# Spectral filter beside a gated MLP: who copies the first transposes, where the next statistics stand, and how wide the first pass is

## Chip, cores, metric

The kernel runs on one core of a Trainium2 chip. The metric is the device time of one execution in microseconds (us). The core has five engines that run their own instruction queues in order and wait for each other through semaphores: TensorE (PE, matrix products, with PEld for its weight loads), VectorE (DVE), ScalarE (ACT), GpSimd (POOL) and SyncE (SP, which here only issues DMA transfers). PE writes to PSUM, a memory of eight banks; a bank must have been read out before PE may write to it again.

## What is computed

The rows of `A_x` (2048 rows of 512) are normalized. The result goes through two branches that are added to `A_x`: a two-dimensional FFT multiplied by a filter and transformed back, and a gated MLP with a tanh GELU.

```python
def _A_ref(x, w_r, w_i):
    B, S, D = x.shape
    X = jnp.fft.rfft2(x.astype(jnp.float32), axes=(-2, -1))
    X = X * (w_r + 1j * w_i)
    return jnp.fft.irfft2(X, s=(S, D), axes=(-2, -1)).astype(jnp.bfloat16)

def _B_ref(x, w_gate, w_up, w_down):
    g = jnp.einsum("bsd,df->bsf", x, w_gate)
    u = jnp.einsum("bsd,df->bsf", x, w_up)
    h = _gelu(g) * u
    return jnp.einsum("bsf,fd->bsd", h, w_down)

x = A_x
xn = _layernorm(x, axis=-1)
return x + _A_ref(xn, A_w_r, A_w_i) + _B_ref(xn, B_w_gate, B_w_up, B_w_down)
```

Here S = 2048, D = 512, and the MLP's inner width is 1792. All data is bfloat16, sums are float32.

## The kernel before

**Tiles.** The 2048 rows are 16 tiles of 128 rows; four tiles make a block of 512. The inner width is 14 slices (`fc`) of 128. A tile is loaded (`load_x`, `load_xc`), its mean and variance are taken on DVE (`ln_stats`, L421 and L422; the second tile in two halves, L428 and L430), the reciprocal root of the variance is formed (tiles 0 and 1: square root on ACT, L433, and reciprocal on DVE, L437; later tiles: POOL, `ln_rstd`, L442 and L443), and the tile is normalized on DVE (`ln_apply`, L450). PE then transposes it in 128 x 128 squares, and the transposed rows are copied from PSUM to `xnT`: tiles 0 and 1 one at a time (`transpose_first`, L465, with the copies at L471 on DVE or L473 on ACT), tiles 2 and 3 together and tiles 4 to 7 together (`transposes`, L490, with one copy on DVE, L497, and one on ACT, L499), later tiles by DMA.

**Units.** A `geglu_unit(b, fc, a, w)` makes `w` columns of slice `fc` of block `b`: four matmuls with the gate weights into one PSUM bank and four with the up weights into the next (both at L561), GELU on ACT from the first bank into a buffer `gg` (L573, three buffers in turn), and the product of that with the second bank on DVE into `hT` (L581). The banks come from a ring: `ring_first` has the six banks 0, 1, 2, 7, 5, 6 in this order, `ring_gu` the three banks 0, 1, 2 from its own start. A unit takes the next two banks of its ring, and waits until what was in them has been read.

**Block 0.** Its rows are not all there at the beginning, so it is done in narrower passes: slices 0 to 2 (`NQUARTER` = 3) on tile 0 alone and then on tile 1 alone, 128 columns each; slices 3 to 6 (up to `NHALF` = 7) on both, 256 columns; then slices 0 to 6 on tiles 2 and 3, 256 columns. The transposes of tiles 2 and 3 come in between, after the unit with `fc == NHALF - 2`. From slice 7 on the units are 512 wide and come from a list (`fillers`), one for each call of `filler()`. After the first of these the four tiles 4 to 7 are normalized, two more follow, and then come the transposes of tiles 4 to 7.

**Weights.** Gate and up weights come in six pieces of columns, `WPIECES` = (0, 128), (128, 384), (384, 640), (640, 896), (896, 1280), (1280, 1792), so slices 7 to 9 lie in piece 4. All loads are issued in a fixed order at the start, most by SP: tiles 0 and 1, gate pieces 0 to 2, and so on down to piece 4 after the four tiles of block 1 (`load_xc(1)`); the first two up pieces are issued by ACT.

**The order of work** is that of the calls at the end of the kernel: each call appends its instructions to the queues of the engines, and each queue is kept in order. ACT's queue at the start: square root for tile 0, square root for tile 1, then a GELU on a single column (L826) whose only purpose is to load the GELU table early, and then the first units' GELUs. PE fills its time before the first tile with 39 matmuls on zeros (`warm_up`, L541).

After block 0's beginning the same list of units is spread between the spectral branch's steps (`unit_A` L634, `unit_d` L660, `unit_B`, `unit_c`, `unit_e`, `unit_fin`), the folds on POOL (`half_fold`, L521) and DVE (`mirror_fold`, L526), and the down projections (L607).

Of the kernel before, what the change touches and what calls it, by code (L numbers as in the profile page):

```python
# [8 lines left out]
ALU = mybir.AluOpType  # L9
# [8 lines left out]
P = 128  # L18
# [209 lines left out]
def bass_parallel_sum__spectral_gfnet__glu_gated_geglu__prompt_kernel(  # L228
# [19 lines left out]
    sch = _Sched()  # L248

    with ExitStack() as es:  # L250

        def sb(name, shape, dt=BF16):
            return es.enter_context(nc.sbuf_tensor(name, shape, dt))
# [6 lines left out]
        hT = [sb("hT%d" % i, [P, NFC, 512]) for i in range(2)]  # L260
# [54 lines left out]
        gu_bank = sp_bank = bank_of  # L315
# [4 lines left out]
        def sp_bank_bf(slot):  # L320
            return ps_bf[:, slot * 1024:(slot + 1) * 1024]
# [6 lines left out]
        ring_first = _Ring((0, 1, 2, 7, 5, 6), bank_readers)  # L328
# [91 lines left out]
        def ln_stats(j):  # L420
            ev = sch.op("dve", lambda e: e.bn_stats(st[:, j, :], x_sb[:, j, :]), deps=[ev_x[j]])  # L421
            ev_ag[j] = sch.op("dve", lambda e: e.bn_aggr(ag[:, j, :], st[:, j, :]), deps=[ev])  # L422
# [3 lines left out]
        def ln_stats_half(h):  # L426

            ev = sch.op("dve", lambda e: e.bn_stats(st1[:, h, :], x_sb[:, 1, h * HD:(h + 1) * HD]), deps=[ev_x[1]])  # L428
            if h == 1:
                ev_ag[1] = sch.op("dve", lambda e: e.bn_aggr(ag[:, 1, :], st1[:]), deps=[ev])  # L430

        def ln_sqrt(a, b):
            return sch.op("act", lambda e: e.activation(rstd[:, a:b], ag[:, a:b, 1], ACT.Sqrt, bias=eps_t[:], scale=1.0),  # L433
                          deps=[ev_ag[b - 1], ev_eps])

        def ln_recip(a, b, ev):
            ev = sch.op("dve", lambda e: e.reciprocal(rstd[:, a:b], rstd[:, a:b]), deps=[ev])  # L437
            for j in range(a, b):
                ev_rstd[j] = ev

        def ln_rstd(a, b):
            ev = sch.op("pool", lambda e: e.tensor_scalar(rstd[:, a:b], ag[:, a:b, 1], LN_EPS, None, ALU.add), deps=[ev_ag[b - 1]])  # L442
            ev = sch.op("pool", lambda e: e.tensor_tensor(rstd[:, a:b], rstd[:, a:b], half_t[:, 0:b - a], ALU.pow), deps=[ev, ev_half])  # L443
            for j in range(a, b):
                ev_rstd[j] = ev
# [3 lines left out]
        def ln_apply(j):  # L449
            ev_xn[j] = sch.op("dve", lambda e: e.tensor_scalar(xn[:, j, :], x_sb[:, j, :], ag[:, j, 0:1], rstd[:, j:j + 1],  # L450
                                                             ALU.subtract, ALU.mult), deps=[ev_rstd[j], ev_ag[j]])

        ev_xnT = {}

        def transpose_first(j, eng):

            evs = []
            for h in range(2):
                slot, bdeps = ring_tr.alloc(1)
                bank = sp_bank_bf(slot)[:, 0:HD].rearrange("p (r s) -> p r s", r=2)  # L460

                def f_tr(e, h=h, bank=bank):
                    ins = None
                    for r in range(2):
                        ins = e.transpose(bank[:, r, :], xn[:, j, (2 * h + r) * P:(2 * h + r + 1) * P], ident)  # L465
                    return ins

                ev_t = sch.op("pe", f_tr, deps=[ev_id, ev_xn[j]] + bdeps)
                dst, src = xnT[:, 2 * h:2 * h + 2, j * P:(j + 1) * P], bank
                if eng == "dve":  # L470
                    ev = sch.op("dve", lambda e, dst=dst, src=src: e.tensor_copy(dst, src), deps=[ev_t])  # L471
                else:
                    ev = sch.op("act", lambda e, dst=dst, src=src: e.activation(dst, src, ACT.Copy), deps=[ev_t])  # L473
                ring_tr.add_reader(slot, ev)
                evs += [ev, ev]
            ev_xnT[j] = evs
# [55 lines left out]
        gg_readers = [[] for _ in range(NGG)]  # L532
        hT_readers = [[], []]
        ev_h_block = {}
# [8 lines left out]

            hT_readers[1].append(sch.op("pe", f, deps=[ev_zero, ev]))

        def geglu_unit(b, fc, a=0, w=512, ring=None):

            k = geg["k"]
            geg["k"] = k + 1
            s2 = k % NGG  # L550
            hb = b % 2
            ring = ring or ring_gu
            pieces = [i for i, (lo, hi) in enumerate(WPIECES) if lo < (fc + 1) * P and fc * P < hi]
            evw, evw_up = ([ev_w[i, q] for i in pieces] for q in range(2))
            evx = [ev_xnT[4 * b + i] for i in range(a // P, (a + w) // P)]
            gslot, gdeps = ring.alloc(1)

            def mm(e, wsb, slot, dcs=range(NDC)):
                ins = None
                for dc in dcs:  # L560
                    ins = e.matmul(gu_bank(slot)[:, 0:w], wsb[:, dc, fc * P:(fc + 1) * P], xnT[:, dc, b * 512 + a:b * 512 + a + w],  # L561
                                   start=(dc == 0), stop=(dc == NDC - 1))
                return ins

            if b == 0 and fc == 0 and a == 0:
                for dc in range(NDC):
                    ev_gm = sch.op("pe", lambda e, dc=dc: mm(e, wg_sb, gslot, (dc,)), deps=evw + [x[dc] for x in evx] + gdeps)
            else:
                ev_gm = sch.op("pe", lambda e: mm(e, wg_sb, gslot), deps=evw + evx + gdeps)
            uslot, udeps = ring.alloc(1)  # L570
            ev_um = sch.op("pe", lambda e: mm(e, wu_sb, uslot), deps=evw_up + udeps)
            gg = gg_sb[s2][:, 0:w]
            ev_gg = sch.op("act", lambda e: e.activation(gg, gu_bank(gslot)[:, 0:w], ACT.Gelu_apprx_tanh),  # L573
                           deps=[ev_gm] + gg_readers[s2])
            gg_readers[s2] = []
            ring.add_reader(gslot, ev_gg)
            hdeps = []
            if fc == 0 and a == 0:
                hdeps = list(hT_readers[hb])
                hT_readers[hb] = []  # L580
            ev_h = sch.op("dve", lambda e: e.tensor_tensor(hT[hb][:, fc, a:a + w], gu_bank(uslot)[:, 0:w], gg, ALU.mult),  # L581
                          deps=[ev_um, ev_gg] + hdeps)
            ring.add_reader(uslot, ev_h)
            gg_readers[s2].append(ev_h)
            ev_h_block.setdefault(b, []).append(ev_h)

        ev_acc = {}

# [224 lines left out]
            finished(j, ev_o)  # L813


        NQUARTER, NHALF = 3, 7
        ln_stats(0)
        ev_sq = ln_sqrt(0, 1)
        ln_stats_half(0)
# [2 lines left out]
            warm_up(n, ev)  # L822
        ln_apply(0)
        ln_stats_half(1)
        ev_sq = ln_sqrt(1, 2)
        sch.op("act", lambda e: e.activation(warm[:], eps_t[:], ACT.Gelu_apprx_tanh), deps=[ev_eps])  # L826
        transpose_first(0, "dve")
        ln_recip(1, 2, ev_sq)
        ln_apply(1)
        for fc in range(NQUARTER):  # L830
            geglu_unit(0, fc, 0, P, ring_first)
            if fc == 0:
                transpose_first(1, "act")
                ln_stats(2)
        ln_stats(3)
        for fc in range(NQUARTER):
            geglu_unit(0, fc, P, P, ring_first)
        ln_rstd(2, 4)
        for fc in range(NQUARTER, NHALF):
            geglu_unit(0, fc, 0, 256, ring_first)  # L840
            if fc == NQUARTER:
                ln_apply(2)
                ln_apply(3)
                half_fold(0)
            if fc == NHALF - 2:
                transposes(2, 4, ring_tr)
# [18 lines left out]
        def filler(n=1):  # L865
            for _ in range(n):
                u = next(fill, None)
                if u is None:
                    return
                todo["left"] -= 1  # L870
                if u[0] == "g":
                    geglu_unit(u[1], u[2])
                else:
                    down_unit(u[1], u[2])

        filler()
        for j in range(4, 8):
            ln_apply(j)
        filler(2)
        transposes(4, 8, ring_tr)  # L880
        half_fold(1)
        filter_i = load_filter("wi", wi_sb, A_w_i)
# [104 lines left out]
```

## Time and profile before

| | us |
|---|---|
| median of 3 runs | 180.57 (180.46 to 180.92) |
| the profiled execution, its time | 179.84 |
| its span, first to last instruction | 178.1 |

| engine | busy us | share of the span |
|---|---|---|
| PE | 174.0 | 98% |
| PEld | 98.6 | 55% |
| DVE | 116.6 | 65% |
| ACT | 87.1 | 49% |
| POOL | 55.1 | 31% |

The 16 DMA engines are busy nine tenths or more of the time in the slices from the second to the tenth (4.45 us a slice), and their rate there is 308 to 379 GB/s for the second to the sixth. A timeline line reads: start, duration, engine, line, operation, output and inputs, shapes, count, and in brackets how long the engine sat idle before it and what ended that. Starts are counted from the span's start. Lines with a `q` behind the engine's name are issues of DMA transfers. Matmul durations overlap; the distance of their starts tells what one costs.

### The profile page before, as it was taken

The page shows a single profiled execution, that of the slowest core. Times are in us where ns is not written, and L with a number is a line of the kernel's source. Part 1 is how long each engine was busy: PE and PEld are TensorE (multiplying, and loading weights), DVE is VectorE, ACT ScalarE, POOL GpSimd, SP SyncE. Part 2 cuts the span into 40 slices and gives each one's busy share as a digit, 9 for nine tenths or more (in the row PEclk, how much of TensorE's full clock was granted, in tenths as well). Part 3 has the DMA queues.
Part 4 walks back from the last instruction along what each step waited for, and adds up shares of the span by engine and source line. Part 5 has one row for each costly group of instructions (what it writes and reads, how often), then busy time and mean ns, then how long its engine had stood idle before and what let it go on. Part 6 is the DMA issues. An engine that isn't in the chain of part 4 may idle for free.

```text
span 178.1 us, 3198 instructions
## 1 busy us (share of the span) xinstructions
PE 174.0 (98%) x1157; PEld 98.6 (55%) x1157; DVE 116.6 (65%) x256; ACT 87.1 (49%) x164; POOL 55.1 (31%) x54
## 2 busy tenths in 40 slices
PE   7899999999999999999999999999999999999995
PEld 7788755555555554444554555554455555555543
DVE  2787986878767636545586886872338868885731
ACT  3635337777463634156374765723166546662100
POOL 0047253326390000000000000000008969997760
PEclk9999999999999999999999999999999999999999
DMA  5999999999997793913344494965500111111101
GB/s 150 308 338 379 372 371 171 199 169 218 231 174 192 143 296 103 305 64 88 94 105 120 91 241 75 243 139 117 118 4 29 59 59 33 60 67 47 39 29 59
DMA packets 38576, 27.15 MB, mean 152 GB/s; under 512 B 7712, under 2 KB 37792, under 8 KB 38432
## 3 DMA queue, kind: packets, MB, share of 16 engines
q1 hardware_dynamic: 34192, 24.95, 56.1%
q10 hardware_dynamic: 4368, 2.00, 5.6%
q8 instruction: 9, 0.15, 0.4%
q14 instruction: 7, 0.06, 0.2%
HBM read 17.48 MB, written 6.30 MB: 134 GB/s over the span
## 4 chain that ended last, share of the span: by engine, by line
PE 94%; ACT 2%; DVE 1%; DMA 1%; issue 0%
PE ps L561 54%; PE ps L607 27%; PE ps L740 2%; PE ps L660 2%; PE ps L634 2%; PE ps L792 2%; PE ps L771 2%; PE ps L709 2%; DMA x_sb<-in_A_x_dram 1%; PE ps L490 1%; ACT L826 1%; DVE st L421 0%; ACT rstd L433 0%; ACT xnT L473 0%; DVE bufA L450 0%
## 5 line engine op out<-in xcount | busy, mean ns | idle before, releaser
L561 PE MATMUL ps<-xnT,wg_sb 128*128 128x512 bf16 (+2 forms) x264 | 59.2, 347 | 0.7 <-DVE xnT L471 0.4
L561 PE MATMUL ps<-xnT,wu_sb 128*128 128x512 bf16 (+2 forms) x264 | 59.2, 347 | 0.2
L581 DVE TENSOR_TENSOR hT<-ps,gg 128x512 bf16<-128x512 f32 (+2 forms) x66 | 39.5, 605 | 23.9 <-PE ps L561 23.0
L607 PE MATMUL ps<-wd_sb,hT 128*128 128x512 bf16 (+2 forms) x238 | 50.7, 366 | 0.0
L573 ACT ACTIVATE gg<-ps 128x512 bf16<-128x512 f32 (+2 forms) x66 | 35.0, 532 | 24.8 <-PE ps L561 21.5
L806 POOL TENSOR_TENSOR bufC<-bufC 128x256 bf16<-128x256 f32 x16 | 14.7, 916 | 84.2 <-DVE bufC L803 84.2
L561 PEld LDWEIGHTS ps<-xnT,wu_sb 128*128 128x128 bf16 x264 | 25.0, 98 | 24.2 <-issue 0.3
L607 PEld LDWEIGHTS ps<-wd_sb,hT 128*128 128x128 bf16 x238 | 22.5, 98 | 23.4
L561 PEld LDWEIGHTS ps<-xnT,wg_sb 128*128 128x128 bf16 x264 | 23.7, 98 | 15.2 <-DMA wg_sb<-in_B_w_gate_dram 0.5
L618 DVE TENSOR_TENSOR x_sb<-ps,x_sb 128x512 bf16<-128x512 f32 (+2 forms) x17 | 11.2, 660 | 24.2 <-PE ps L607 24.2
L521 POOL TENSOR_TENSOR bufC<-bufA 128x1024 bf16<-128x1024 bf16 x8 | 16.8, 2124 | 8.6 <-DVE bufA L450 8.6
L810 POOL TENSOR_TENSOR x_sb<-x_sb,bufC 128x512 bf16<-128x512 bf16 x16 | 18.7, 1169 | 2.3
L745 ACT ACTIVATE Vp<-ps 128x514 bf16<-128x514 f32 x16 | 9.5, 599 | 15.3 <-PE ps L740 15.3
L776 ACT ACTIVATE bufA<-ps 128x512 bf16<-128x512 f32 x16 | 9.4, 597 | 14.6 <-PE ps L771 14.6
L668 ACT ACTIVATE bufB<-ps 128x512 bf16<-128x512 f32 x16 | 11.9, 744 | 9.5 <-PE ps L660 9.5
L421 DVE BATCH_NORM_STATS2 st<-x_sb 128x6 f32<-128x512 bf16 x15 | 10.2, 683 | 2.3 <-DMA x_sb<-in_A_x_dram 2.3
L802 DVE TENSOR_TENSOR bufC<-bufC,ps 128x256 f32<-128x256 f32 x16 | 6.7, 421 | 5.3 <-ACT bufC L799 5.3
L641 ACT ACTIVATE tmp<-ps 128x512 bf16<-128x512 f32 x9 | 5.4, 597 | 6.1 <-PE ps L634 6.1
L442 POOL TENSOR_SCALAR rstd<-ag 128x4 f32<-128x4 f32 (+1 forms) x4 | 1.3, 316 | 21.3 <-DVE ag L422 21.3
L714 ACT ACTIVATE Xc<-ps 128x514 bf16<-128x514 f32 x12 | 7.0, 595 | 1.0 <-PE ps L709 1.0
L799 ACT ACTIVATE bufC<-ps 128x256 f32<-128x256 f32 x16 | 6.0, 378 | 2.6 <-PE ps L792 2.6
L806 DVE TENSOR_TENSOR bufC<-bufC 128x256 bf16<-128x256 f32 x16 | 6.8, 424 | 0.5
(52 smaller groups left out, 137.5 us busy)
## 6 DMA issues: line engine op xcount, KB each, us to landing
stage_g<-Vp SPq DMA_DIRECT2D x16, 128.5 KB, 3.3
bufC<-stage_p SPq DMA_DIRECT2D x4, 512.0 KB, 5.2
out_dram<-x_sb SPq DMA_DIRECT2D x15, 128.0 KB, 1.7
wd_sb<-in_B_w_down_dram SPq DMA_DIRECT2D x1, 1792.0 KB, 15.3
stage_p<-bufB SPq DMA_DIRECT2D x7, 256.0 KB, 5.7
wr_sb<-in_A_w_r_dram SPq DMA_DIRECT2D x6, 257.0 KB, 10.7
wi_sb<-in_A_w_i_dram SPq DMA_DIRECT2D x6, 257.0 KB, 10.2
JX<-Xc SPq DMA_DIRECT2D x24, 64.2 KB, 2.6
```

The source lines that it names most:

```text
L421: ev = sch.op("dve", lambda e: e.bn_stats(st[:, j, :], x_sb[:, j, :]), deps=[ev_x[j]])
L521: ev_hf[m] = [sch.op("pool", lambda e, t=t, op=op: e.tensor_tensor(half[:, m, t, :, :], rows[:, 0, :, :], rows[:, 1, :, :], op), deps=deps ...
L561: ins = e.matmul(gu_bank(slot)[:, 0:w], wsb[:, dc, fc * P:(fc + 1) * P], xnT[:, dc, b * 512 + a:b * 512 + a + w], start=(dc == 0), stop=(d ...
L573: ev_gg = sch.op("act", lambda e: e.activation(gg, gu_bank(gslot)[:, 0:w], ACT.Gelu_apprx_tanh), deps=[ev_gm] + gg_readers[s2])
L581: ev_h = sch.op("dve", lambda e: e.tensor_tensor(hT[hb][:, fc, a:a + w], gu_bank(uslot)[:, 0:w], gg, ALU.mult), deps=[ev_um, ev_gg] + hdeps)
L607: ins = e.matmul(bank(slot)[:, 0:w], hT[hb][:, fc, jj * P:(jj + 1) * P], wd_sb[:, fc, cs], start=(fc == 0), stop=(fc == NFC - 1))
L618: ev_a = sch.op("dve", lambda e, slot=slot, cs=cs, w=w: e.tensor_tensor(x_sb[:, j, cs], bank(slot)[:, 0:w], x_sb[:, j, cs], ALU.add), deps ...
L668: ev_T[j] = sch.op("act", lambda e: e.activation(dst, src, ACT.Copy), deps=[ev_p])
L745: ev_v = sch.op("act", lambda e: e.activation(Vp[sv][:], sp_pair(slot), ACT.Copy), deps=[ev_p] + Vp_readers[sv])
L776: ev_ZT[j] = sch.op("act", lambda e: e.activation(ZT[:, :, j, :], src, ACT.Copy), deps=[ev_p] + [ev_xnT[i][0] for i in (11, 15)])
L806: y = [sch.op(("dve", "pool")[h], lambda e, h=h, op=op: e.tensor_tensor(rS[s2][:, h * HD:(h + 1) * HD], yeS[s2][:, 0, :], yeS[s2][:, 1, :] ...
L810: ev_o = sch.op("pool", lambda e: e.tensor_tensor(x_sb[:, j, :], x_sb[:, j, :], rS[s2], ALU.add), deps=[a, b, ev_xn[j]] + ev_acc.get(j, []))
```

## The change

Four edits in block 0 (line numbers of the functions behind it shift by 2 to 7).

- `transpose_first` takes one engine for each of a tile's two copies. Tile 0's are now copied by ACT and DVE (before: both by DVE), tile 1's by DVE both (before: both by ACT). Tile 0's call moves ahead of the second tile's square root in the order of calls.
- `geglu_unit` can hand its product back instead of appending it (`late=True`). The first unit's product is appended after tile 1's copies, so that DVE has the copies first.
- The statistics of tiles 2 and 3 move on DVE's queue: from behind the first and the third product to behind the fourth and the sixth.
- `NHALF` is 8 instead of 7: slice 7 of block 0 is done in two units of 256 columns in the passes instead of one of 512. The transposes of tiles 2 and 3 stand one unit later with it. One unit fewer is left in the list, and `filler(2)` ahead of the transposes of tiles 4 to 7 becomes `filler()`.

```diff
-        def transpose_first(j, eng):
+        def transpose_first(j, engs):
 
             evs = []
-            for h in range(2):
+            for h, eng in enumerate(engs):
...
-        def geglu_unit(b, fc, a=0, w=512, ring=None):
+        def geglu_unit(b, fc, a=0, w=512, ring=None, late=False):
...
-            hdeps = []
-            if fc == 0 and a == 0:
-                hdeps = list(hT_readers[hb])
-                hT_readers[hb] = []
-            ev_h = sch.op("dve", lambda e: e.tensor_tensor(hT[hb][:, fc, a:a + w], gu_bank(uslot)[:, 0:w], gg, ALU.mult),
-                          deps=[ev_um, ev_gg] + hdeps)
-            ring.add_reader(uslot, ev_h)
-            gg_readers[s2].append(ev_h)
-            ev_h_block.setdefault(b, []).append(ev_h)
+
+            def product_h():
+                hdeps = []
+                if fc == 0 and a == 0:
+                    hdeps = list(hT_readers[hb])
+                    hT_readers[hb] = []
+                ev_h = sch.op("dve", lambda e: e.tensor_tensor(hT[hb][:, fc, a:a + w], gu_bank(uslot)[:, 0:w], gg, ALU.mult),
+                              deps=[ev_um, ev_gg] + hdeps)
+                ring.add_reader(uslot, ev_h)
+                gg_readers[s2].append(ev_h)
+                ev_h_block.setdefault(b, []).append(ev_h)
+
+            if late:
+                return product_h
+            product_h()
...
-        NQUARTER, NHALF = 3, 7
+        NQUARTER, NHALF = 3, 8
...
         ln_stats_half(1)
+        transpose_first(0, ("act", "dve"))
         ev_sq = ln_sqrt(1, 2)
         sch.op("act", lambda e: e.activation(warm[:], eps_t[:], ACT.Gelu_apprx_tanh), deps=[ev_eps])
-        transpose_first(0, "dve")
         ln_recip(1, 2, ev_sq)
         ln_apply(1)
-        for fc in range(NQUARTER):
+        product_h = geglu_unit(0, 0, 0, P, ring_first, late=True)
+        transpose_first(1, ("dve", "dve"))
+        product_h()
+        for fc in range(1, NQUARTER):
             geglu_unit(0, fc, 0, P, ring_first)
-            if fc == 0:
-                transpose_first(1, "act")
-                ln_stats(2)
-        ln_stats(3)
         for fc in range(NQUARTER):
             geglu_unit(0, fc, P, P, ring_first)
+            if fc in (0, 2):
+                ln_stats(2 + fc // 2)
         ln_rstd(2, 4)
...
         filler()
         for j in range(4, 8):
             ln_apply(j)
-        filler(2)
+        filler()
         transposes(4, 8, ring_tr)
```

## Prediction

> **What bounds the kernel now.** I read the page first (busy shares, chain), then the windows, then the chain and the timeline of the first 30 us, where every edit lies.
>
> ```profile
> span 178.1 us, 3198 instructions
> PE 94%; ACT 2%; DVE 1%; DMA 1%; issue 0%
> ```
>
> ```profile
> 14.00:22.00 8.00, 8.00 (x68) 6.32 (x66) 7.01 (x18) 3.54 (x9) 3.81 (x4) 1.00 1.06 377
> ...
> 27.00:175.00 148.00, 148.00 (x912) 78.09 (x911) 96.20 (x200) 74.85 (x136) 45.58 (x41) 1.00 0.56 124
> ```
>
> In the windows the first number after the length is PE's busy time: from 14 us on PE is busy 8.00 of 8.00 and 148.00 of 148.00 us. So whatever PE's queue gains or loses in the first 27 us reaches the end nearly whole, and all that counts is when PE issues. The chain of waits from 5 to 30 us shows where PE does stand still:
>
> ```profile
> 5.99 1.28 ACT L826
> ...
> 7.65 0.56 ACT xnT L473 x2
> 8.21 0.05 issue
> 8.26 0.64 PE ps L561 x8
> 8.89 0.27 DVE hT L581
> 9.16 0.05 issue
> 9.21 1.28 PE ps L561 x16
> 10.49 0.07 issue
> 10.56 2.34 PE ps L561 x20
> ```
>
> Comparing PE's starts with its pitch (0.056 us for a 128-column matmul, 0.109 for 256, from back-to-back starts) gives stalls of 0.53 (before 6.02, for the first tile's copies), 0.21 (before 6.68, second tile's normalization), 0.45 (before 8.26: ACT copies the second tile, behind the table load), 0.27 (9.21: a product freeing its PSUM bank), 0.23 (10.56: the same, the product queued behind statistics) and 0.07 (14.13).
>
> **The change, part by part.** Times are those of the profiled execution.
>
> *First tile, one copy each.* The first pair of transposes releases its copy at 5.56. Now that copy is DVE's, over at 5.87, the second one at 6.07. On ACT such a copy takes 0.38 (L473), so it ends about 5.95, DVE's about 6.03. The first product starts 0 to 0.08 later than at 6.02: no gain. The copy now sits ahead of the second square root on ACT: back-to-back copies start 0.26 apart, so the root moves from 5.68 to 5.84, and the reciprocal, the second normalization and its transposes by 0.16; the table load and first GELU move by the same 0.16.
>
> *Second tile on DVE, before the first product.* Transposes at 6.84, DVE copies (0.29, pitch 0.21) end at about 7.7, while PE works on units 1 and 2 until 7.97 (3 units of 8 x 0.056). The 0.45 wait is gone: the second quarter starts at 7.97 instead of 8.26. With the statistics behind the fourth and sixth products, the 0.27 and 0.23 waits go as well: the sixth unit ends at 9.31, where now unit four of the wide kind starts at 9.89. A gain of 0.58 so far, and 0.81 after the 10.56 wait is gone.
>
> *Statistics later.* The third tile's now begin after the fourth product, about 9.0, the fourth's after the sixth, about 10.2 to 11.1 (0.69 + 0.18 each); POOL's rstd (1.04 from 10.32 to 11.36 now) ends about 12.2, the two normalizations (0.72) at 13.0. The transposes moved one unit later in the loop (`NHALF - 2` is now 6) would be reached by PE at 12.81, so they wait 0.26, to 13.07, and end at 13.51.
>
> *Eight units in the first pass: the weight piece.* Next on PE is unit fc=7 on tiles 0 and 1, formerly first touched at 20.24. It lies in weight piece 4 (columns 896 to 1280), whose DMAs are issued and land thus (issue times from the timeline, last column of the DMA view is us to landing):
>
> ```profile
> 7.26 0.43 SPq L341 DMA_DIRECT2D wg_sb<-in_B_w_gate_dram  x1
> 7.74 0.70 SPq L341 DMA_DIRECT2D wu_sb<-in_B_w_up_dram  x1
> ```
>
> ```profile
> wg_sb<-in_B_w_gate_dram SPq DMA_DIRECT2D x1, 384.0 KB, 6.3
> wu_sb<-in_B_w_up_dram SPq DMA_DIRECT2D x1, 384.0 KB, 7.0
> ```
>
> Gate weights land at 13.6, up weights at 14.75. Nothing that the change touches is ahead of them in SP's or ACT's queue, so they land then again. PE would want the up weights at 14.08: it waits to about 14.80, the up product takes 4 x 0.109, and the second pass starts at 15.24. Before it started at 14.13 with half a unit (0.87) less done: 15.24 - 0.87 - 14.13 = +0.24 us late. The whole gain of the opening (0.81, less 0.26) is swallowed, and any slip there below 0.67 would be too.
>
> The rate behind it: in the window 2.20 to 14.75 the DMA engines moved 323 GB/s at a busy share above 1. The Trainium skill ("Perfetto Trace Analysis", Roofline) puts one core's ceiling at about 435 GB/s; by that the same bytes would be there at about 11.5 and the wait would not exist (an estimate from that page). The trace's landing decides against it.
>
> *Eight units: PSUM bank.* The second pass is 8 units of 0.87: 15.24 + 6.98 = 22.22, against 21.97 before for the same work (fc 0 to 7 whole; the eighth as two halves costs 1.75 instead of 1.73). The next unit, fc=8, takes ring banks 0 and 1 from the start of `ring_gu`. `ring_first` has six banks in turn, two a unit: before, 17 units left banks 0 and 1 to the last but one; now the 19th unit, just finished, has them. So fc=8 waits for that unit's GELU. In the profile
>
> ```profile
> 14.13 0.60 PE L561 MATMUL ps<-xnT,wg_sb 128*128 128x256 bf16 x4
> ...
> 14.77 0.38 ACT L573 ACTIVATE gg<-ps 128x256 bf16<-128x256 f32 x1 [0.50 <-PE ps L561]
> ```
>
> a unit's GELU ends 1.02 after its gate starts; with 0.05 to PE that is 1.07, the unit is 0.87: +0.20. fc=8 starts at 22.42, 0.45 late.
>
> *`filler(2)` becomes `filler()`: normalizations 4 to 7.* They stand in DVE's queue behind the product of the unit before. Then PE had two 512-wide units until the transposes, now one:
>
> ```profile
> 20.24 1.03 PE L561 MATMUL ps<-xnT,wg_sb 128*128 128x512 bf16 x4
> ...
> 22.17 0.69 DVE L581 TENSOR_TENSOR hT<-ps,gg 128x512 bf16<-128x512 f32 x1
> ...
> 22.78 1.37 DVE L450 TENSOR_SCALAR bufA<-x_sb,ag,rstd 128x512 bf16<-128x512 bf16 x4
> ...
> 25.42 1.06 PE L490 MATMUL ps<-small,bufA 128*128 128x128 bf16 x16
> ```
>
> A wide unit's product starts 1.93 after the unit (20.24 to 22.17), the last normalization ends 1.98 after that, 0.05 to PE: 3.96. Two wide units take 3.45 (21.97 to 25.42). Now the transposes come just two units after fc=8 starts: they are reached at 25.87 and ready at 22.42 + 3.96 = 26.38: a wait of +0.51, where before there was a cover of 20.24 + 3.96 = 24.20 against 25.42, 1.2 us. DVE's queue bears this: the two mirror folds ahead (1.29) end by 24.2, before the product at 24.35. POOL's rstd for these tiles (1.04) ends about 22.5, in time.
>
> **Sum:** +0.24 (weights) + 0.20 (bank) + 0.51 (normalizations) = +0.95, with nothing after it to take it back. Profiled execution: span 178.1 + 0.95 = 179.05; its time 179.84 + 0.95 = 180.8. The median shown is 180.57, 0.73 above the profiled one, so 181.5. The bounds of the unknown: the landing can shift (at 14.0 or earlier, limited by tile 2 and 3's copies at 14.5, the first term becomes -0.50; 0.5 later, +0.74); the last two terms stand on durations of the same instructions and I give them 0.1 each.
>
> **Rivals.** This kernel's measurement tells about 0.3% (0.54 us) from no change.
>
> 1. *The up weights come in time* (by 14.0). Place: the tenth unit; it decides from 14.75 - 14.0 = 0.7 us earlier landing. Then the second pass starts at 14.5: -0.50 + 0.20 + 0.51 = +0.2, 180.8: not slower by what can be told. For it: unprofiled executions need not have this landing. Against: 323 GB/s at full DMA share, and no transfer ahead was removed. 0.16.
> 2. *The transposes don't wait*, because DVE gets to the normalizations half a microsecond sooner: +0.45, 181.0. For it: nothing but that product and folds overlap by 0.1 each. Against: DVE takes its queue in order, the product waits for PE. 0.06.
> 3. *The opening's gain reaches the end*: the 0.81 saved up to 10.56 stays on PE's queue, and neither later wait shows because the landing is early and DVE keeps its old cover: 179.8. It needs piece 4 by 13.5, and the fence above shows that cover taken away. 0.04.
> 4. *PE's clock falls in the new stalls.* The profile grants full clock in all 40 slices; the warm-up matmuls from 0.97 to about 5.0 run at 0.107 pitch, half speed, so one more such stretch costs 2 us: 183.5. Against: the 0.53 stall before 6.02 is followed by 0.056 pitch at once, and the new ones are 0.7 and 0.5. 0.03. The Trainium skill ("TensorE: Matmul & The Clock Gate", Part 1) puts the drop behind an idle window of about 3.4 us, but also reports micro-idles between groups as a second cause; by the first rule there is none here, by the second the rival's 2 us.
>
> **How the numbers follow.** The forecast has 0.71 and is 181.5, its own spread 181.1 to 182.0. The range reaches to rival 1's 180.8 and upward to 182.1 for a landing 0.5 later. Slower: the forecast, rival 4 and a little of rival 2, 0.76; same: the rest of rivals 1 and 2, 0.19; faster: rival 3 and the lower edge of 1, 0.05.
>
> **What would show it.** Right: the second quarter at about 8.0 with no ACT copy before it; PE idle before the up matmuls of the tenth unit, released by the up weights near 14.8; a gap of 0.2 before the first 512-wide unit, released by ACT's GELU; a gap of 0.5 before the 16 transposes, released by DVE L450, near 26.4. From there every PE start about 0.95 later than before. Wrong: piece 4 landed before 14.1, or the transposes follow the matmuls without a gap.

## The result, and the profile after

The changed kernel takes 181.65 us (median of 6 runs, 181.52 to 182.02), the kernel before 180.78 beside it (6 runs, 180.46 to 181.0): a ratio of 1.0052, 95% interval 1.0038 to 1.0066. The forecast was 181.5. Here and below the ratio is not the quotient of the two medians; it differs from it by up to 0.0013. Ratios leave out two executions in a slow state, one of e2 (184.27) and one of e8 (183.58).

The profiled execution of the changed kernel took 181.52, its span is 179.7. That of the kernel before, 179.84, lies below all six of its runs (180.46 to 181.0); the 1.6 us between the two spans is therefore not the effect. This matters below.

The page's head after, then the waits of PE from 12 to 30 us (who waited for what: us in total, times, longest):

```profile
span 179.7 us, 3217 instructions
...
PE 89%; SPq 4%; DMA 4%; DVE 1%; issue 0%
```

```profile
PE ps L561 <- DMA wu_sb<-in_B_w_up_dram: 0.5, 1, 0.5
PE ps L490 <- DVE bufA L450: 0.3, 1, 0.3
PE ps L561 <- DMA wg_sb<-in_B_w_gate_dram: 0.3, 1, 0.3
```

The chain that ended last now has 4% of issues on SP's queue and 4% of a weight load in it, which it had not before. The chain of waits from 5 to 30 us shows where:

```profile
8.34 0.04 issue
8.38 7.05 DMA wu_sb<-in_B_w_up_dram
15.43 0.04 issue
15.48 7.60 PE ps L561 x68
23.07 0.04 issue
23.11 1.92 PE ps L561 x8
25.03 0.02 issue
25.05 0.69 DVE hT L583
25.74 0.82 DVE bufA L450 x3
26.57 0.06 issue
26.62 0.42 DVE bufA L450
27.04 0.05 issue
27.09 1.07 PE ps L490 x16
```

Read from the top: the up weights of piece 4, issued at 8.38, land at 15.43; PE goes on at 15.48. Then 68 matmuls without a stop, a break until 23.11, one 512-wide unit, and the chain leaves PE: the unit's product on DVE, the normalizations behind it, and only then the transposes. PE's timeline at these three places:

```profile
14.39 0.61 PE L561 MATMUL ps<-xnT,wg_sb 128*128 128x256 bf16 x4 [0.35 <-DMA wg_sb<-in_B_w_gate_dram]
...
15.48 0.61 PE L561 MATMUL ps<-xnT,wu_sb 128*128 128x256 bf16 x4 [0.48 <-DMA wu_sb<-in_B_w_up_dram]
15.92 0.60 PE L561 MATMUL ps<-xnT,wg_sb 128*128 128x256 bf16 x4
...
22.47 0.60 PE L561 MATMUL ps<-xnT,wu_sb 128*128 128x256 bf16 x4
...
23.11 1.04 PE L561 MATMUL ps<-xnT,wg_sb 128*128 128x512 bf16 x4
...
25.71 1.03 PE L561 MATMUL ps<-xnT,wu_sb 128*128 128x512 bf16 x4
...
27.09 1.07 PE L490 MATMUL ps<-small,bufA 128*128 128x128 bf16 x16 [0.35 <-DVE bufA L450]
```

The brackets count from a matmul's modelled end; from the starts the stalls are longer. The last unit's up matmuls start at 22.47 and need 4 x 0.109: 22.91, and the next start is 23.11, so 0.20. The up matmuls at 25.71 need 4 x 0.216: 26.57, next start 27.09, so 0.51 (with unrounded starts). The tenth unit waits twice for weights of piece 4: its gate matmuls, reached at 13.87 (8 transposes of 0.056 from 13.42 on), start at 14.39, so 0.52; its up matmuls, reached at 14.39 + 4 x 0.109 = 14.83, start at 15.48, so 0.64.

Where the rest of the time went is quickly told. From the transposes of tiles 4 to 7 to the end of the span it is 152.6 to 152.7 in this profile (179.7 - 27.09), in the first one of the kernel before (178.1 - 25.42), and in eight of the twelve experiments' profiles. What the change does is done by then. The other four are e5 to e8, which ran on one chip (153.0 to 154.2): there PE stood still once more near 131 us, for 0.37 to 1.24, for a transfer of the spectral branch.

| profiled execution | PE continues with piece 4's up weights | transposes 4 to 7 start | span | rest |
|---|---|---|---|---|
| before | (needs them after 21) | 25.42 | 178.1 | 152.7 |
| before, second profile (e5) | (needs them after 21) | 26.08 | 179.1 | 153.0 |
| before, loads swapped (e11) | (needs them after 21) | 26.13 | 178.8 | 152.7 |
| changed | 15.48 | 27.09 | 179.7 | 152.6 |
| changed, second profile (e9) | 15.77 | 27.38 | 180.0 | 152.6 |
| weights first (e1) | 14.24, no wait | 25.91 | 178.6 | 152.7 |
| banks (e2) | 16.76 | 29.83 | 182.5 | 152.7 |
| normalizations first (e3) | 16.62 | 27.72 | 180.4 | 152.7 |
| banks and normalizations (e10) | 15.41 | 26.30 | 178.9 | 152.6 |
| all three (e4) | 16.33, no wait | 27.27 | 179.9 | 152.6 |
| all three, old opening (e12) | 15.23, no wait | 26.17 | 178.8 | 152.6 |
| all three, statistics earlier (e8) | 15.56, no wait | 26.51 | 180.1 | 153.6 |
| opening only (e6) | (needs them after 22) | 26.80 | 180.5 | 153.7 |
| passes only (e7) | 15.66, no wait | 27.32 | 181.5 | 154.2 |

In e2, e4, e7 and e8 PE ran at half speed for a stretch in these first 30 us, beyond the warm-up (told below), so their starts can't be compared with the others'.

### The profile page after: what moved, and what is told of

Same layout as the page of the kernel before. It is cut to its first block, busy times and chain, and to the rows that moved or that the text cites. A ratio compares the mean times of both kernels' runs of the same rounds, so it can differ in the third digit from the quotient of the medians.

```text
span 179.7 us, 3217 instructions
## 1 busy us (share of the span) xinstructions
PE 174.6 (97%) x1165; PEld 99.3 (55%) x1165; DVE 117.3 (65%) x258; ACT 87.4 (49%) x164; POOL 55.1 (31%) x54
## 4 chain that ended last, share of the span: by engine, by line
PE 89%; SPq 4%; DMA 4%; DVE 1%; issue 0%
PE ps L561 49%; PE ps L613 27%; SPq L341 4%; DMA wu_sb<-in_B_w_up_dram 4%; PE ps L746 2%; PE ps L798 2%; PE ps L777 2%; PE ps L666 2%; PE ps L640 2%; PE ps L715 2%; DVE bufA L450 1%; PE ps L490 1%; DVE hT L583 0%; DVE x_sb L624 0%
```

## The experiments

They ran on three chips in sets of four (e1 to e4, e5 to e8, e9 to e12); each ratio is against the kernel before on the same chip, whose medians there are 180.55, 181.35 and 180.66. Only the third set has the changed kernel beside it.

**e1: piece 4 ahead of the tiles of block 1**

```diff
         load_w(3)
-        load_xc(1)
         load_w(4)
+        load_xc(1)
```

> The changed kernel, with weight piece 4 issued ahead of the four tiles of block 1 (512 KB). Theory (three separate waits, about 0.24 + 0.20 + 0.51 us): in the changed kernel's trace the tiles land at 13.2 and the up weights at 15.4; swapped, the up weights land about 13.9, the wait of 0.64 before the up matmuls and that of 0.5 before the gate matmuls go, and the second pass is held by the copies of tiles 2 and 3 near 14.7 instead of starting at 15.9. 0.7 to 1.2 us off the changed kernel's 181.65: 180.5 to 180.95, ratio to the kernel before 0.998 to 1.001; the waits of 0.20 and 0.51 stay. Rival (one delay seen three times: the late start is what makes the two later waits): the two later waits shrink too, and the ratio falls to 0.996 or less.

Measured: 180.53, ratio 1.0004 (0.9983 to 1.0025). Of PE's waits from 12 to 30 us that this view lists one is left, and the second pass starts at 14.75:

```profile
PE ps L490 <- DVE bufA L450: 0.3, 1, 0.3
```

```profile
13.35 0.62 PE L490 MATMUL ps<-small,bufA 128*128 128x128 bf16 x8
13.80 0.60 PE L561 MATMUL ps<-xnT,wg_sb 128*128 128x256 bf16 x4
14.24 0.60 PE L561 MATMUL ps<-xnT,wu_sb 128*128 128x256 bf16 x4
14.75 0.60 PE L561 MATMUL ps<-xnT,wg_sb 128*128 128x256 bf16 x4
```

The later waits stay at 0.20 and 0.51 although everything is 1.2 earlier (transposes at 25.91 against 27.09). They are waits of their own, not one delay seen three times.

**e2: the ring of three banks starts at its third**

```diff
+        ring_gu.pos = 2
         filler()
         for j in range(4, 8):
             ln_apply(j)
```

> The changed kernel, with the ring of three banks started at its third bank, so that the first 512-wide unit doesn't take the bank whose GELU is still running. Theory: the gap of 0.20 before that unit goes and everything behind it comes 0.20 earlier: 181.45, ratio 1.004; the waits for the weights and of 0.51 before the transposes stay. Rival (one delay seen three times): the gap goes but PE waits that much longer at the transposes, 181.65, ratio 1.005.

Measured: 181.34, ratio 1.0042 (1.0024 to 1.0061). The stall before the first 512-wide unit is gone, the next start being 4 x 0.109 behind:

```profile
25.43 0.60 PE L561 MATMUL ps<-xnT,wu_sb 128*128 128x256 bf16 x4
25.86 1.03 PE L561 MATMUL ps<-xnT,wg_sb 128*128 128x512 bf16 x4
```

The one before the transposes stays 0.51. The interval holds 1.004 and 1.005 alike, so the trace settles this, not the time. The profiled execution was the longest of the twelve; this place lies behind what made it long.

**e3: the normalizations ahead of the 512-wide product**

```diff
-        filler()
         for j in range(4, 8):
             ln_apply(j)
-        filler()
+        filler(2)
```

> The changed kernel, with the four normalizations of tiles 4 to 7 ahead of the first 512-wide product on DVE's queue instead of behind it; PE's order is untouched. Theory: the normalizations end near 26.2 on the changed kernel's time axis, before PE's 26.6, the wait of 0.51 goes and nothing takes its place: 181.15, ratio 1.002. Rival: the product, now 1.3 late, holds a PSUM bank and the wait only moves to the next units: 181.5 to 181.7, ratio 1.004 to 1.005.

Measured: 181.52, ratio 1.0054 (1.0034 to 1.0073). By its time the rival wins; its trace says otherwise. There PE's transposes follow without a wait (up matmuls at 26.85, 4 x 0.216 later the transposes at 27.72) and no other wait takes its place:

```profile
PE ps L561 <- DMA wu_sb<-in_B_w_up_dram: 1.6, 1, 1.6
PE ps L561 <- DMA wg_sb<-in_B_w_gate_dram: 0.2, 1, 0.2
```

From the up matmuls of the tenth unit to the transposes it is 27.72 - 16.62 = 11.10, in the changed kernel 27.09 - 15.48 = 11.61: 0.51 less. But the up weights landed 1.1 later in this execution than in the changed kernel's. If they did so in most of its runs, that hides the gain; only one execution was profiled, and at 182.15 it was the longest of its eight, so this is not shown. The changed kernel wasn't run on this chip, either. e10 asks again.

**e4: the three edits together** (no diff of its own)

> All three edits together. Theory (three separate waits): their gains add, 0.7 to 1.2 + 0.20 + 0.51 = 1.4 to 1.9 us off 181.65: 179.7 to 180.25, ratio 0.994 to 0.997, faster than the kernel before, since the opening's own gain is then left over. Rival (one delay seen three times): no further than the first edit alone brings it.

Measured: 179.96, ratio 0.9978 (0.9954 to 1.0003). The view of PE's waits from 12 to 30 us is empty: no stall before the 512-wide unit, none before the transposes of tiles 4 to 7. For the weights this profile is no test, since it is the longest of the twelve (181.7): PE ran at half clock until 11.97 and came to the tenth unit's up matmuls at 16.33, with the weights there since 14.71. By time the version is 0.6 us below e1, where 0.71 was expected, and seven of its twelve runs lie below e1's lowest (180.02). That speaks for gains that add and against the rival's "no further", though the two intervals overlap, and the ratio is just above the 0.994 to 0.997 that was expected. Whether it beats the kernel before its interval leaves just open; it is the fastest version measured.

**e5: the kernel before, once more** (unchanged)

> The kernel before, unchanged, as one more kernel: it gives a second profile of it beside its first one, which at 179.84 was 0.9 below the median of its other runs. Theory (the landing of the weight loads moves from execution to execution, and the kernel before meets that in its opening): ratio 1.000, single runs over about 1 us of range; in this profile weight piece 1 and the up weights of piece 4 land 0.3 to 0.7 later than 6.7 and 14.75, PE waits for piece 1 before its second unit, the second pass starts later than 14.13 by that much, and no wait longer than 0.15 is seen behind it. Rival (the first profile is typical, and the 0.9 lies outside the span): same landings within 0.1, second pass at 14.1.

Measured: ratio 0.9998 (0.9973 to 1.0024), runs from 180.41 to 182.28, a range of 1.9 where about 1 was expected. The second pass starts at 14.79 instead of 14.13. Piece 1's gate weights landed at 7.39 instead of 6.73, the third tile at 8.69 instead of 8.03, and DVE shows what that does:

```profile
7.75 0.29 DVE L581 TENSOR_TENSOR hT<-ps,gg 128x128 bf16<-128x128 f32 x1 [1.15 <-ACT gg L573]
8.72 0.69 DVE L421 BATCH_NORM_STATS2 st<-x_sb 128x6 f32<-128x512 bf16 x1 [0.67 <-DMA x_sb<-in_A_x_dram]
9.45 0.18 DVE L422 BATCH_NORM_AGGREGATE ag<-st 128x2 f32<-128x6 f32 x1
9.54 0.47 DVE L581 TENSOR_TENSOR hT<-ps,gg 128x128 bf16<-128x128 f32 x2
```

In the old order the third tile's statistics stand between the first product and the second. They wait 0.67 for the tile, and with them the products whose banks PE needs: PE stops until 9.87. The theory had not named this stop (PE came to it at 9.02, so 0.85). The up weights of piece 4 landed at 15.94, 1.2 later than in the first profile, where 0.3 to 0.7 was said, and one stall is behind it that was not expected: 0.37 near 131 us, where PE waits for a transfer of the spectral branch that held PE up in no profile of the other chips.

**e6: the new opening alone**

```diff
-        NQUARTER, NHALF = 3, 8
+        NQUARTER, NHALF = 3, 7
...
-        filler()
+        filler(2)
         transposes(4, 8, ring_tr)
```

> The changed kernel with the passes of before: NHALF back to 7 and two units ahead of the transposes of tiles 4 to 7; only the edits to the opening remain. Theory: PE reaches the transposes of tiles 2 and 3 a unit earlier, at about 12.3 of the changed kernel's axis, with the normalizations over at 13.4, so a wait of about 1.1 stands there and the opening's 0.8 is lost to it; no wait for piece 4, none of 0.20, none of 0.51. The second pass starts near 14.4 to 14.7: 0 to 0.4 slower than before, ratio 1.000 to 1.002. Rival (the opening's gain is real and only the eight units ruin it): 0.5 to 0.8 faster, ratio 0.995 to 0.997.

Measured: 181.8, ratio 1.0027 (0.9996 to 1.0058). No gain, as the theory says, with the new wait in its place: matmuls at 12.56 that need 0.44, and then

```profile
14.12 0.62 PE L490 MATMUL ps<-small,bufA 128*128 128x128 bf16 x8 [0.95 <-DVE bufA L450]
```

which is a stall of 1.12. The rival's 0.995 to 0.997 is outside the interval. The time alone wouldn't settle it: from the transposes of tiles 4 to 7 on this profile takes 153.7, e5's 153.0, because PE stands still for 0.5 more behind DVE (L734). Up to there the trace agrees: from the first product to these transposes it is 26.80 - 7.00 = 19.80, in e5 26.08 - 6.32 = 19.76. So the new opening needs the later place of the transposes of tiles 2 and 3, and that came with the eight units.

**e7: the new passes alone** (the kernel before with `NHALF` 8 and `filler()`)

> The kernel before with only the passes changed: NHALF 8 and one unit ahead of the transposes of tiles 4 to 7; copies and statistics as before. Theory: the wait for the up weights of piece 4 levels both openings, so this is the changed kernel's time: ratio 1.004 to 1.006, waits for piece 4, of 0.20 and of 0.51 in the trace. Rival (the new opening is worth something in the changed kernel): slower than the changed kernel by 0.3 to 0.8, ratio 1.007 to 1.010.

Measured: 183.29, ratio 1.0096 (1.0058 to 1.0134): in the rival's range. The waits of 0.20 and 0.51 are there. But the profiled execution started 128-column matmuls at a distance of 0.107 instead of 0.056 until 10.4, so that it came to the up weights of piece 4 at 15.66, as they landed, and it lost 1.24 (by the starts) to a late transfer:

```profile
PE ps L771 <- DMA bufB<-stage_g: 1.1, 1, 1.1
```

The profile of e8, another kernel on this chip, has both too, so neither need belong to the edit. The changed kernel alone came out at 1.0086 on another chip (e9), with overlapping intervals, so whether the old opening costs more here is not decided. The granted clock of the windows reads 1.00 in that slow start, as it does during the warm-up matmuls; only the distance of the starts shows it.

**e8: e4 with the fourth tile's statistics behind the fifth product**

```diff
-            if fc in (0, 2):
-                ln_stats(2 + fc // 2)
+            if fc < 2:
+                ln_stats(2 + fc)
```

> The three edits of the fourth experiment, and the fourth tile's statistics one product earlier (behind the fifth instead of the sixth). Theory: the wait of 0.24 before the transposes of tiles 2 and 3 (seen at 13.4 in the changed kernel) shrinks to nothing, and the second pass, which waits for their copies, starts 0.2 earlier where the weights allow it: 179.75 to 179.95, ratio 0.995 to 0.998, faster than the kernel before. Rival (the weights' landing holds the start of the second pass anyway): as the fourth experiment, 0.998.

Measured: 181.33, ratio 0.9995 (0.9967 to 1.0023). That is above what both the theory and the rival said, though its interval holds them in part. Its profile has the doubled distance until 10.3 and a stall of 0.94 at 131 us, too, so the point itself was not tested.

**e9: the changed kernel once more** (unchanged)

> The changed kernel, unchanged, once more, so that the next kernels stand beside it on the same chip. Theory: ratio to the kernel before 1.004 to 1.006; the three waits again in the profile, that of 0.20 and that of 0.51 the same to 0.02, the one for the up weights of piece 4 of another length, since their landing moved between 14.75 and 16.7 in the profiles so far. Rival (the two later waits depend on the late start): they differ with it.

Measured: 181.98, ratio 1.0086 (1.0058 to 1.0114), above what was expected. Its stalls: 0.71 for the up weights (PE goes on at 15.77), 0.21 before the 512-wide unit once a matmul missing from the records there is allowed for, and 0.51 before the transposes. The theory's fixed waits are fixed, and the rival is out. The up weights landed at 15.72 in this execution, 0.29 later than in the changed kernel's first profile; e10's landed at 15.36 on the same chip. What makes 0.6 us of difference between the ratios 1.0052 and 1.0086 is open.

**e10: e2 and e3 together, loads in their own order**

> The changed kernel with the second and the third experiment's edits and the loads in their own order: the two later waits are gone, the one for the weights stays. Theory: 0.71 off, ratio 1.004 to 1.006 less 0.0039: 1.000 to 1.002; from the start of the second pass to the end of the span 163.1 us (before: 163.05 for the same work; changed: 163.81). Rival (the third experiment's 1.0054: taking the wait away brings nothing): 1.004 or more.

Measured: 181.03, ratio 1.0018 (0.9998 to 1.0038), beside e9's 1.0086. The waits from 12 to 30 us:

```profile
PE ps L561 <- DMA wu_sb<-in_B_w_up_dram: 0.6, 1, 0.6
PE ps L561 <- DMA wg_sb<-in_B_w_gate_dram: 0.2, 1, 0.2
```

From the up matmuls of the tenth unit to the transposes: 26.30 - 15.41 = 10.89, against 11.61 in the changed kernel's both profiles (27.38 - 15.77). That is 0.72, where 0.20 + 0.51 was worked out. In the medians it is 0.95 (181.98 - 181.03); the first products and the up weights came earlier in e10's profile than in e9's. The second pass to the end takes 178.9 - 15.86 = 163.0, as was expected (163.1).

**e11: the kernel before with e1's loads**

> The kernel before with the loads of the first experiment (weight piece 4 ahead of the four tiles of block 1), a control for it. Theory: the kernel before needs piece 4 only at about 20 us, and the statistics that need the tiles start at 15.6 and have time: ratio 0.999 to 1.001. Rival (the order of loads is better for any of these kernels, and the first experiment shows nothing of this wait): 0.994 to 0.996, as much as it took off the changed kernel.

Measured: 180.47, ratio 0.9991 (0.9976 to 1.0006). The order of loads does nothing for the kernel before that could be told, so what e1 gained is the wait for piece 4.

**e12: e4 with the old opening**

> The fourth experiment with the opening of before: eight units in the first pass and the three edits (loads, banks, normalizations), but the copies and statistics of before. Theory: with the weights in time, what is left of the new opening is 0.2 to 0.25 (second pass at 14.7 by the copies of tiles 2 and 3, against 14.9): ratio 0.998 to 1.000. Rival (the new opening keeps its whole 0.8): 1.002 to 1.003.

Measured: 180.59, ratio 1.0001 (0.9986 to 1.0016), at the theory's upper edge, with the rival's 1.002 just outside. The trace speaks for the rival. The old opening again stops PE, for 0.83, until the products behind the third tile's statistics are done, and the second pass starts late:

```profile
9.92 0.40 PE L561 MATMUL ps<-xnT,wu_sb 128*128 128x128 bf16 x4 [0.67 <-DVE hT L581]
...
15.74 0.60 PE L561 MATMUL ps<-xnT,wg_sb 128*128 128x256 bf16 x4
```

The theory had put it at 14.9; by the first profile of the kernel before it would be 14.13 + 0.87 = 15.0. With the new opening and the same loads it was 14.75 (e1): 1.0 earlier after the same eight units, 0.17 of it from an earlier first product. By time e4 stands 0.0023 below, which is 0.4 us, on another chip and with overlapping intervals. So the traces show the new opening ahead at the second pass once the weights are there; what it is worth at the end is open.

## Why the prediction was right, point by point

*PE's queue decides, and only its first 27 us.* Shown: the rest is 152.6 to 152.7 in both profiles of the changed kernel, the first of the kernel before and all of the first and third set. The second set (e5 to e8) adds stalls of 0.4 and more near 131 us.

*First tile, one copy each: no gain.* Right: the first product starts at 6.11 (0 to 0.08 after 6.02 was said), the table load at 6.16 instead of 5.99.

*Second tile and statistics.* The mechanism holds: no wait for ACT's copy and none for a product up to the tenth unit. The second quarter starts at 8.34 and not at 7.97, because the second unit's gate weights landed at 7.39 in this execution (6.73 in the first of the kernel before):

```profile
7.44 0.40 PE L561 MATMUL ps<-xnT,wg_sb 128*128 128x128 bf16 x4 [0.20 <-DMA wg_sb<-in_B_w_gate_dram]
```

The wait before the transposes of tiles 2 and 3 was put at 0.26 and is 0.24.

*The weights.* Here a premise failed: "they land then again". The up weights landed at 15.43, not at 14.75, the gate weights at 14.34, not at 13.6, and in the other profiles with this order of loads the up weights came at up to 16.7. The term was still about right, since the loads of the opening were later by the same (0.66 for piece 1 and the third tile, 0.68 for these) and held up the kernel before as well: second pass at 14.79 in e5 and 14.84 in e11, so 15.92 - 0.87 - 14.84 = 0.21 against a like execution, where 0.24 was said. Taken against the first profile it would be 0.92. That the two shifts match was not foreseen and is luck: with the changed kernel's second profile it is 16.21 - 0.87 - 14.84 = 0.50, and in e3 the up weights were 1.1 later at nearly the same opening. The mechanism, the wait for piece 4, is shown by experiment: without it (e1) the transposes start 1.18 earlier and the ratio is 1.0004 instead of 1.0052 (on another chip), while the same order of loads gains nothing for the kernel before (e11).

*The bank.* 0.20 said, 0.20 seen: ACT's GELU of the last 256-wide unit runs from 22.67 to 23.05, and PE goes on at 23.11. The wait goes with the ring's start (e2) and stays when all else is earlier (e1).

*The normalizations.* 0.51 said, 0.51 seen, gone in e3 and e10 with nothing in its place.

*The sum.* Said 0.95, measured 0.87 in the medians; the transposes start at 27.09 against 26.08 (e5), which is 1.0. Adding it to the median rather than to the profiled 179.84 was what made the time right: that execution had the earliest landing of these weights, and the sum from it was 180.8.

*Rivals.* The first, weights in time, is what e1 made: 1.0004, the "not slower" that was worked out for it. The second, transposes that don't wait, is out: they waited 0.51 in both profiles. The third, the opening's gain reaching the end, didn't come about; with all three waits taken away the ratio is 0.9978, whose interval just holds 1 (e4). The fourth, PE at half clock, was given 0.03: no sign in the changed kernel's two profiles, but one of e9's six runs (182.13) has a mean granted clock of 0.991, like the two executions shown below.

## What to carry to other kernels

Before a loop is widened over more of an operand, look when that part of the operand lands: a wait there levels everything that was saved ahead of it. A count that is moved from one loop to the next (here a unit from the list into the passes) shifts ring positions and takes away the cover of what was queued by position; follow both. One profile of a kernel that starts on saturated loads is one draw: take a second before terms of a few tenths are read from the landing times.

## What the runs showed of the hardware

**Landings move.** The same queue of loads in the same order, some 4 MB in the first 15 us, brought the up weights of piece 4 at 14.75, 15.36, 15.43, 15.62, 15.72, 15.94, 16.09, 16.57 and 16.72 in nine profiled executions. In six of them (the first two profiles, e6, e7, e9, e10) the transfer took 6.9 to 7.1 from its issue, and what moved was the issue on SP's queue, from 7.74 to 9.02: SP spent longer on the issues ahead. One of them, in the kernel before and then in the changed kernel:

```profile
5.26 1.19 SPq L341 DMA_DIRECT2D wu_sb<-in_B_w_up_dram  x1
```

```profile
5.26 1.73 SPq L341 DMA_DIRECT2D wu_sb<-in_B_w_up_dram  x1
```

In e5, e3 and e2 the transfer itself took longer as well, 7.6, 8.2 and 8.6. Why the issues take longer at times is open.

**PE's clock falls after less than an idle window.** In e2's profiled execution, which took 184.27, PE stood still for 2.08 before 16.76. Windows of 3.41 us before and after (PE busy first, the granted clock third from the end):

```profile
13.50:16.91 3.41, 1.09 (x12) 0.60 (x10) 0.98 (x3) 0.98 (x2) 3.41 (x2) 1.00 1.04 383
16.91:20.33 3.42, 3.42 (x18) 2.44 (x17) 1.32 (x3) 0.43 (x2) 0.52 (x1) 0.50 1.10 363
```

The clock was halved for exactly this window, though PE had been busy for 1.09 us of the one before. In e4's profiled execution (181.7, the longest of its twelve) it happened after 1.74 us of work in a window:

```profile
5.14:8.55 3.41, 1.74 (x27) 1.38 (x26) 1.99 (x8) 2.25 (x6) 0.00 (x0) 1.00 1.14 321
8.55:11.97 3.42, 3.42 (x36) 3.42 (x34) 1.85 (x6) 1.30 (x5) 0.00 (x0) 0.50 1.15 308
```

The Trainium skill ("TensorE: Matmul & The Clock Gate", Part 1) has the windows of 3.41 us, which these rows bear out, and the drop after an idle window, which is too narrow by them if it means a window without any work. e3's execution idled for 1.65 before 16.62 and kept its clock, so the limit is not found here. For this kernel it means that a late weight load can cost more than its wait. How often can be estimated: one such window at half clock (1.7 us lost of 180) makes the mean granted clock of an execution 0.99, as it is in these two (0.991), and 15 of the 223 runs on record with a clock have 0.990 or 0.991, 7 of them among the 101 of the kernel before. Whether a late load is behind each of them is not known.
